# Splitting the first group's triangular inverse between VectorE and TensorE

## The chip, the cores and the metric

The kernel runs on one core of one Trainium2 chip. A core has five engines that each take their own queue of instructions: TensorE (PE, matrix products; PEld is its loading of weights), VectorE (DVE), ScalarE (ACT), GpSimd (POOL) and SyncE (SP, here only the issuing of transfers). The metric is the device time of one execution in microseconds (us). Line numbers such as L507 are those of the kernel before; the changed kernel has its own, some 40 to 60 higher from the place of the first edit on.

## What is computed

The reference is a linear attention with a delta rule, followed by a mixture of experts over slots. Only the first half is touched by the change.

```python
for t in range(S):                       # S = 768 tokens, B = 4, H = 8, D = 48
    kt, vt, bt = (k_n[:, :, t], v[:, :, t], beta[:, :, t, None])     # k_n: normed keys
    y[:, :, t] = np.einsum('bhd,bhde->bhe', q[:, :, t], state)
    v_old = np.einsum('bhde,bhd->bhe', state, kt)
    state = state + bt[:, :, :, None] * np.einsum('bhd,bhe->bhde', kt, vt - v_old)
...
logits = x @ phi                         # x: y as (3072, 384); 32 slots
d = softmax over tokens;  slot_input = d.T @ x;  relu(slot_input @ w1) @ w2 per expert
c = softmax over slots;   out = c @ slot_out
```

The 768 steps are worked in chunks of 32 tokens. Within a chunk the steps depend on each other through a lower triangular 32x32 system for each of the 32 pairs of batch and head. With its inverse T in hand, a chunk is a handful of matrix products: R = v minus keys times state, U = T R, state plus keys times U, and outputs from the state and from U.

## The kernel before, in words

**Chunks, slots and groups.** There are NCH = 24 chunks. The loop `for x in range(NCH)` treats one chunk in each turn, called a slot. Four chunks make a group (GC = 4, NG = 6), and one inverse covers a whole group: the 128 partitions hold 4 heads x 32 rows, and VectorE inverts for all of them at once. `U` = 8 pairs of batch and head-half lie in the free dimension of each chunk.

**The inverse, `invert(n)`.** `unit` and `clear` zero two scratch tiles on GpSimd (`tt`, and `nm` inside `prs`). `spread` (L325) transposes the products of keys with keys, `GQ`, in blocks of 32, `root` has ScalarE take the norms, and `norms` scales the system. `steps` is a list of small VectorE operations. The triangle is cut into halves of HC = 16: `ea`/`es` (an outer product at L368 and its subtraction at L373) solve both diagonal halves together; `ma`/`ms` and `la`/`ls` build the block that couples them, in `nm` and `T21`, and `join` (L410) copies it into `tt`. `back(half)` (L433) transposes half of the columns into `TT[n]`, as the solves want it. Before the first slot the steps of group 0 run in one go; those of later groups are dealt out over the four slots before they are needed, by `plan(n)` and the table `share`, in three places of each slot. A first argument of `put` weighs each step by its size.

**A chunk's slot.** In the order in which each engine's queue receives it: `rest` (state times keys into `psR`, and R, by VectorE or, where `turned_sign` holds, by a TensorE product with `minus`, L494, and a ScalarE copy, L498), `read` (state times queries, L481), `solve` (L507, with the matrices `Tb` that `solvers` has ScalarE make from `TT`, L458; ScalarE copies U, L510), then preparation of later chunks by `later(x, place)`, then `update` (L520, with the state's copy at L527) and `outputs` (L537, copied at L540). `Prep` turns keys and queries on TensorE (L261) into `KQ` (ScalarE copies at L270 and L277) and multiplies them (`products`, L290, copies at L294). Until slot 3 the table `ahead` names what is prepared where: q2 is query 2's turn, p2 its products, t8 and u8 the two halves of chunk 8's turns. All of these products share two PSUM buffers, the tag `pt`. `weights` masks the query products on GpSimd (L450), and `scale_v` scales the values there (L442).

**What sets the order.** The region is under a manual schedule: each engine runs its instructions in the order in which the code issues them, and waits by semaphores for its operands and for buffers. Transfers of keys, queries and values are issued by SyncE, four for each load (L93), in order too; a load into a buffer in use holds up those behind it.

**Routing.** `route(n, ...)` returns what a finished group contributes to the experts' slots, as lists by slot and place (`hook`). `shares` is four small VectorE operations (L638 to L641), `collect` adds up the slots' inputs. The weights of the experts are loaded during the later slots into what comes free; their products run after the last slot.

Of the kernel before, what the change touches and what calls it, by code (L numbers as in the profile page):

```python
# [9 lines left out]
F32 = mybir.dt.float32  # L10
AX = mybir.AxisListType
ALU = mybir.AluOpType
# [5 lines left out]
def kernel(  # L18
# [26 lines left out]
    nc = tc.nc  # L45
# [58 lines left out]
    def load_q(cc, eng=nc.sync):  # L104
        load(q, q_of(cc), cc, eng)
# [196 lines left out]
    def invert(n):  # L302
# [72 lines left out]
        def steps():  # L375

            pr, out = {}, []

            def put(size, f):
                out.append((60 + size, f))  # L380

            def ea(j):
                lb, tt, m, w = part(st["lb"]), part(st["tt"]), j + 1, HC - 1 - j
                pr["e", j] = outer("prE", [2, w, m], tt[:, :, j, 0:m].unsqueeze(2),
                                   lb[:, :, j, j + 1:HC].unsqueeze(3))

            def es(j):
                add(part(st["tt"])[:, :, j + 1:HC, 0:j + 1], pr["e", j], ALU.subtract)

            def ma(j):  # L390
                lb, tt, m = full(st["lb"]), full(st["tt"]), j + 1
                pr["m", j] = outer("prM", [HC, m], tt[:, j, 0:m].unsqueeze(1),
                                   lb[:, j, HC:C].unsqueeze(2))

            def ms(j):
                add(nm[:, :, 0:j + 1], pr["m", j], ALU.subtract)

            def la(j):
                a, b = full(st["tt"])[:, HC + j:C, HC + j].unsqueeze(2), nm[:, j, :].unsqueeze(1)
                if j == 0:  # L400
                    nc.vector.tensor_tensor(T21, a.broadcast_to([P, HC, HC]),
                                            b.broadcast_to([P, HC, HC]), op=ALU.mult)
                else:
                    pr["l", j] = outer(("prE", "prM")[j % 2], [HC - j, HC], a, b)

            def ls(j):
                add(T21[:, j:HC, :], pr["l", j], ALU.add)

            def join():
                nc.vector.tensor_copy(full(st["tt"])[:, HC:C, 0:HC], T21)  # L410

            for j in range(HC):
                last = j == HC - 1
                if not last:
                    put(2 * (j + 1) * (HC - 1 - j), lambda j=j: ea(j))
                put(HC * (j + 1), lambda j=j: ma(j))
                if not last:
                    put(2 * (j + 1) * (HC - 1 - j), lambda j=j: es(j))
                put(HC * (j + 1), lambda j=j: ms(j))
            for j in range(HC + 1):  # L420
                if j < HC:
                    put(HC * (HC - j), lambda j=j: la(j))
                if j > 1:
                    put(HC * (HC + 1 - j), lambda j=j - 1: ls(j))
            put(HC * HC, join)
            return out

        def back(half):

            if n not in TT:  # L430
                TT[n] = lp.tile([P, C, C], F32, name="TT", tag="TT", bufs=2)
            r = slice(half * HC, (half + 1) * HC)
            nc.vector.transpose(TT[n][:, :, r].rearrange("p c i -> p i c"), full(st["tt"])[:, r])  # L433

        return dict(unit=unit, clear=clear, spread=spread, root=root, norms=norms, back=back,
                    steps=steps())
# [128 lines left out]
    def route(n, Yn, yT, cs=range(GC), turn=None, behind=False):  # L565
# [160 lines left out]
    def drain(ls):  # L726
        for f in ls:
            f()
# [11 lines left out]
    PLACES = 3  # L740
    share = [(0.0, 0.05, 0.11), (0.0, 0.14, 0.15), (0.13, 0.10, 0.10), (0.12, 0.10, 0.0)]

    def plan(n):

        f = invert(n)
        at = [[[] for _ in range(PLACES)] for _ in range(GC)]
        todo, done, total = f["steps"], 0.0, 0.0
        whole = sum(t[0] for t in todo)
        norms = f["norms"]
        i = 0  # L750
        for c in range(GC):
            for p in range(PLACES):
                total += share[c][p] * whole
# [10 lines left out]
    nc.vector.tensor_reduce(msk, msk4, axis=AX.X, op=ALU.add)  # L764
    order = tc.manual_schedule()
    order.__enter__()

# [15 lines left out]
    f0["norms"]()  # L783
    pre[0].alone(1, 0)
    load_q(7)
    f0["clear"]()
    drain([t[1] for t in f0["steps"]])
    for i in range(2):
        f0["back"](i)
    pre[0].products(1, 2)  # L790
    scale_v(0)
    for cc in range(4, 8):
        pre[cc] = Prep(cc)
        pre[cc].alone(0, 1)
        pre[cc].alone(1, 0)
        if cc > 4:
            pre[cc - 1].products()
    load_q(1)
    load_k(8)
    load_q(2)  # L800
    load_q(8)
    load_q(3)
# [12 lines left out]
    f["unit"]()  # L815
    f["clear"]()
    routing, yT, two = {}, {}, {}


    def step(cc, kind):  # L820
# [61 lines left out]
    for x in range(NCH):  # L882
        n, c = divmod(x, GC)
        if c == 0 and n:
            routing[n - 1] = route(n - 1, Ys[(n - 1) % 2], yT[n - 1])

        def hook(name):
            for m in sorted(routing):
                at = x - GC * (m + 1)
                if at < len(routing[m]):  # L890
                    drain(routing[m][at].get(name, []))
            if x >= NCH - 2:
                ends(x, name)


        if x + AHEAD < NCH:
            load_k(x + AHEAD)
        for i in queries.get(x, (x + AHEAD,)):
            if i < NCH:
                load_q(i)  # L900
        if 0 <= x + 4 < NCH:
            load_v(x + 4)
        if 8 <= x < 8 + NKT:
            if x == 8:
                w0 = wpool.tile([P, NKT * F], F32, name="w0", tag="w0", bufs=1)
# [31 lines left out]
        later(x, 1)  # L937
        hook("mid")
# [239 lines left out]
```

## Time and profile before

| what | value |
|---|---|
| time, median of 3 runs | 314.1 us (313.29 to 319.79) |
| span of the profiled execution | 310.8 us, mean TensorE clock 0.945 |
| busy: PE / DVE / ACT / POOL | 84% / 70% / 55% / 51% |
| chain that ended last: PE / DVE / ACT | 47% / 24% / 16% |
| first group's inverse on VectorE, L368 to L410 | 19.2 to 39.6 us |
| first solve of slots 0, 1, 2, 3, 4 (L507) | 42.8, 57.3, 66.3, 75.3, 84.8 us |

Busy shares are means over the whole span, and the stages differ. The chain of waits goes back from the last instruction through whatever released each step, so that it says for each stretch of time which engine set the pace. The rows by stage give the clock that was granted to TensorE, 1.00 being full speed. A matrix product of 32-bit numbers shows as two records in the profile, so a group of 32 products is listed as x64.

### The profile page before, as it was taken

Reading aid. Unit: us, or ns where it says so; the run is one execution under the profiler, and the core shown is the slowest. Engines: PE = TensorE matmul, PEld = TensorE weight load, DVE = VectorE, ACT = ScalarE, POOL = GpSimd, SP = SyncE. Lnnn points to the kernel's source line nnn. Section 1 sums busy time; section 2 is a strip of 40 time slices with the busy share of each in tenths; the row PEclk is TensorE's granted clock in tenths of the full one; section 3 lists DMA queues with packets and bytes.
Section 4 is the critical chain, followed back from the end, with each engine's and each line's share of the span. In section 5 each row is a group of like instructions: output and inputs, shape, how many; then the busy total and the mean of one; then the engine's idle time right before and its main releaser. Section 6 shows DMA issues by size and latency. Waiting matters only on the chain.

```text
span 310.8 us, 16635 instructions
## 1 busy us (share of the span) xinstructions
PE 261.1 (84%) x7081; PEld 209.0 (67%) x7081; DVE 216.3 (70%) x807; ACT 171.7 (55%) x386; POOL 159.2 (51%) x336
## 2 busy tenths in 40 slices
PE   3996848998898988999988999796998878999981
PEld 2764636787787777777877877675877666447750
DVE  7689957969489995999579996999832223124341
ACT  3355236476777668578685678556576642211231
POOL 8969094861749957873789509999420000000000
PEclk9999566999999999999999999999799998999985
DMA  7765555434545444665431365668786599591387
GB/s 142 147 112 89 90 96 98 75 60 82 88 72 85 80 79 67 138 135 129 77 83 31 89 165 188 182 183 246 239 263 206 166 344 345 180 308 57 119 262 232
DMA packets 96378, 45.28 MB, mean 146 GB/s; under 512 B 75440, under 2 KB 89808, under 8 KB 96304
## 3 DMA queue, kind: packets, MB, share of 16 engines
q1 hardware_dynamic: 94512, 42.98, 55.3%
q0 software_dynamic: 704, 1.03, 1.5%
q8 instruction: 56, 0.92, 1.2%
q10 hardware_dynamic: 1088, 0.20, 0.3%
q14 instruction: 18, 0.15, 0.2%
HBM read 39.47 MB, written 4.72 MB: 142 GB/s over the span
## 4 chain that ended last, share of the span: by engine, by line
PE 47%; DVE 24%; ACT 16%; issue 3%; DMA 3%; SPq 2%; POOL 2%; DVEq 0%; POOLq 0%; ACTq 0%
DVE prs L368 9%; PE psR L507 6%; DVE prs L373 5%; PE psS L520 5%; PE pt L290 5%; ACT S L527 4%; PE pso L1061 3%; PE ph L1038 3%; PE pt L558 3%; PE pt L261 3%; DVE tt L373 3%; PE psY L537 2%; ACT dr L678 2%; PE psR L481 2%; PE po L1119 2%
## 5 line engine op out<-in xcount | busy, mean ns | idle before, releaser
L442 POOL TENSOR_SCALAR Vs<-Vs,nT 128x48 f32<-128x48 f32 x192 | 89.7, 491 | 22.9 <-DMA Vs<-in_v_dram 6.9
L373 DVE TENSOR_TENSOR prs<-prs 128x16 f32<-128x16 f32 (+15 forms) x186 | 55.8, 300 | 0.4
L450 POOL TENSOR_SCALAR_AFFINE_SELECT Abs<-GQ 32x256 f32<-32x256 f32 x96 | 48.5, 505 | 14.0 <-PE psY L537 9.2
L368 DVE TENSOR_TENSOR prs<-tt,lb 128x96 f32<-128x96 f32 (+21 forms) x186 | 47.8, 295 | 0.1
L527 ACT ACTIVATE S<-psS 48x768 f32<-48x768 f32 x46 | 36.9, 802 | 5.5 <-PE psS L520 5.0
L507 PE MATMUL psR<-R,Tbs 64*64 64x48 f32 x768 | 28.6, 226 | 11.8 <-ACT R L498 8.3
L507 PEld LDWEIGHTS psR<-R,Tbs 64*64 64x64 f32 x768 | 25.7, 140 | 15.6 <-ACT R L498 10.0
L290 PE MATMUL pt<-KQ 48*32 48x64 f32 (+1 forms) x1792 | 26.0, 234 | 5.4 <-ACT KQ L277 3.2
L510 ACT ACTIVATE U<-psR 128x384 f32<-128x384 f32 x24 | 11.8, 490 | 32.4 <-PE psR L507 27.2
L290 PEld LDWEIGHTS pt<-KQ 48*32 48x32 f32 x1792 | 21.0, 117 | 10.4 <-ACT KQ L277 5.0
L537 PE MATMUL psY<-U,Abs 64*64 64x48 f32 x768 | 27.4, 220 | 0.2 <-issue 0.2
L368 DVE TENSOR_TENSOR prs<-tt,prs 128x240 f32<-128x240 f32 (+14 forms) x90 | 27.0, 306 | 0.0
L537 PEld LDWEIGHTS psY<-U,Abs 64*64 64x64 f32 x768 | 24.3, 134 | 2.8 <-issue 0.7
L373 DVE TENSOR_TENSOR tt<-tt,prs 128x30 f32<-128x30 f32 (+7 forms) x90 | 26.0, 288 | 0.0
L458 ACT ACTIVATE Tbs<-TT,own 128x256 f32<-128x256 f32 x48 | 21.6, 501 | 5.9 <-DVE TT L433 5.9
L294 ACT ACTIVATE GQ<-pt 128x256 f32<-128x256 f32 (+1 forms) x56 | 16.9, 351 | 12.8 <-PE pt L290 12.5
L481 PEld LDWEIGHTS psR<-S,KQ 128*32 128x32 f32 x768 | 16.4, 112 | 8.8 <-ACT S L527 4.6
L481 PE MATMUL psY<-S,KQ 128*32 128x96 f32 x768 | 21.5, 246 | 1.0 <-issue 0.8
L481 PE MATMUL psR<-S,KQ 128*32 128x96 f32 x768 | 21.2, 253 | 1.0 <-ACT S L527 0.8
L558 PE MATMUL pt<-ident,Y 128*96 128x128 f32 x96 | 16.4, 294 | 6.4 <-ACT GQ L294 5.7
L500 DVE TENSOR_TENSOR R<-Vs,psR 128x384 f32<-128x384 f32 x14 | 7.7, 553 | 18.7 <-PE psR L481 7.1
L320 POOL MEMSET prs<- 128x256 f32 x6 | 1.9, 315 | 34.8 <-DVE prs L368 34.8
(230 smaller groups left out, 598.9 us busy)
## 6 DMA issues: line engine op xcount, KB each, us to landing
Q<-in_q_dram SPq DMA_DIRECT2D x96, 48.0 KB, 2.6
wKQ<-in_moe_w_dram SPq DMA_DIRECT2D x16, 256.0 KB, 3.9
Vs<-in_v_dram SPq DMA_DIRECT2D x80, 48.0 KB, 2.4
wGQ<-in_moe_w_dram SPq DMA_DIRECT2D x12, 256.0 KB, 4.8
Ka<-in_k_dram SPq DMA_DIRECT2D x40, 48.0 KB, 2.5
w<-in_moe_w_dram SPq DMA_DIRECT2D x6, 256.0 KB, 3.9
Ka<-in_moe_w_dram SPq DMA_DIRECT2D x8, 192.0 KB, 3.8
S<-in_moe_w_dram SPq DMA_DIRECT2D x8, 192.0 KB, 5.2
```

The lines of the kernel that those rows point to most:

```text
L290: nc.tensor.matmul(pg[g][rh, b], lhsT=kq[r, b, 0, rh], rhs=kq[r, b, a0:a1, rh], start=True, stop=True, skip_group_check=True)
L294: nc.scalar.activation(GQ[n][:, c, :, g, a0:a1], pg[g], ACT.Copy)
L368: nc.vector.tensor_tensor(pr, a.broadcast_to([P] + shape), b.broadcast_to([P] + shape), op=ALU.mult)
L373: nc.vector.tensor_tensor(dst, dst, pr, op=op)
L442: nc.gpsimd.tensor_scalar(Vt[cc][:, u], Vt[cc][:, u], nT[n][:, c * U + u:c * U + u + 1], None, op0=ALU.mult)
L450: nc.gpsimd.affine_select(out=Ab[cc % NT][r, :, h % 2, :].rearrange("p (b g) t -> p b g t", g=G), in_=GQ[n][r, c, :, :, 1, :], compare_op= ...
L458: nc.scalar.activation(Tb[cc % 2][:, :, x, :], TT[n][:, c * U:(c + 1) * U, :], ACT.Identity, scale=own[:, x:x + 1])
L481: nc.tensor.matmul(dst[hs[h], b].rearrange("p g d -> p (g d)"), lhsT=kq[:, b, a, hs[h]], rhs=old[:, h, b, :], start=((a == 1 or not turned ...
L507: nc.tensor.matmul(pw[half[y], u], lhsT=T[y][:, u], rhs=st["R"][half[y], u], start=(u == 0), stop=True, skip_group_check=True)
L527: nc.scalar.activation(new[r, :, :, g * D:(g + 1) * D], psS[r, :, 0:B * GD].rearrange("p h (b g e) -> p h b g e", b=B, g=G)[:, :, :, g], A ...
L537: nc.tensor.matmul(qs[half[y], b, g], lhsT=at[y][:, u], rhs=st["U"][half[y], u], start=False, stop=True, skip_group_check=True)
L558: nc.tensor.transpose(py[:, b, :], Yn[:, c, i + b, 0:GD], ident)
```

## The change

For group 0 alone, VectorE now solves only the two diagonal halves. The coupling block of each chunk is made by TensorE: `inner` multiplies the key products by the second half of the inverse, ScalarE copies the result with its sign turned, `outer` multiplies the first half's rows into it, and VectorE adds the result to `TT[0]`. For this the first half is also needed untransposed by columns: `rows` makes it in a scratch, `w0`, that the experts' weights use later. Chunk 0 is coupled ahead of slot 0, the other three in the slots before they are needed. The aim is a shorter stretch in which VectorE alone is at work ahead of slot 0.

Along with it, `spread` and `root` of group 1 move ahead of slot 0 and its steps get a table of their own, `first`; query 1's preparation moves into slot 0, and those of queries 2 and 3 later by a place or a slot; query loads are issued at other points; and `shares` of a group's routing moves from behind `collect(True)` to an earlier place of the same slot.

```diff
@@ steps()
+            if n == 0:
+                for j in range(HC - 1):
+                    put(2 * (j + 1) * (HC - 1 - j), lambda j=j: ea(j))
+                    put(2 * (j + 1) * (HC - 1 - j), lambda j=j: es(j))
+                return out
...
+        def rows(dst):
+            nc.vector.transpose(dst[:, :, 0:HC].rearrange("p c k -> p k c"),
+                                full(st["tt"])[:, :, 0:HC].rearrange("p i k -> p k i"))
...
+    class Coupling:
+        def each(self, lhsT, rhs):
+            p = pt([P, U, HC])
+            for u in range(U):
+                for h in range(4):
+                    r = slice(C * h, C * h + C)
+                    nc.tensor.matmul(p[r, u], lhsT=lhsT(r, u), rhs=rhs(r, u), start=True,
+                                     stop=True, skip_group_check=True)
+            return p
+        def inner(self):
+            p = self.each(lambda r, u: GQ[0][r, self.c, u // G, u % G, 0, :],
+                          lambda r, u: TT[0][r, self.c * U + u, HC:C])
+            nc.scalar.activation(self.sums[:, self.us], p, ACT.Copy, scale=-1.0)
+        def outer(self):
+            self.p = self.each(lambda r, u: self.rows[r, self.c * U + u],
+                               lambda r, u: self.sums[r, self.c * U + u])
+        def add(self):
+            o = TT[0][:, self.us, HC:C]
+            nc.vector.tensor_tensor(o, o, self.p, op=ALU.add)
@@ route()
-                    dict(sums=[lambda: slots((0, 1))], vec=[lambda: collect(True), shares]),
+                    dict(sums=[lambda: slots((0, 1))], act=[shares],
+                         vec=[lambda: collect(True)]),
@@ plan(), for n == 1
+    first = [(0.0, 0.10, 0.15), (0.0, 0.12, 0.13), (0.12, 0.10, 0.10), (0.10, 0.08, 0.0)]
@@ ahead of slot 0
+    w0 = wpool.tile([P, NKT * F], F32, name="w0", tag="w0", bufs=1)
...
+    nc.gpsimd.memset(w0[:, 0:C * C], 0.0)
...
-    f0["clear"]()
-    drain([t[1] for t in f0["steps"]])
-    for i in range(2):
-        f0["back"](i)
     pre[0].products(1, 2)
     scale_v(0)
+    load_k(8)
+    drain([t[1] for t in f0["steps"]])
+    f0["back"](1)
+    f0["rows"](rows11)
+    f0["back"](0)
+    couple = [Coupling(c, rows11, sums21) for c in range(GC)]
     for cc in range(4, 8):
         pre[cc] = Prep(cc)
         pre[cc].alone(0, 1)
+        if cc == 7:
+            couple[0].inner()
         pre[cc].alone(1, 0)
...
-    pre[7].products()
-    pre[1].alone(1, 0)
-    pre[1].products(1, 2)
+    couple[0].outer()
+    couple[0].add()
     weights(0)
     solvers(0)
+    pre[7].products()
+    couple[1].inner()
     scale_v(1)
...
     f["clear"]()
+    f["spread"]()
+    f["root"]()
...
-    ahead = {0: ("q2 p2", "t8 u8", "q3 p3"), 1: ("p8", "t9 u9", "p9"),
+    ahead = {0: ("q1 p1", "t8 u8", "q2 p2"), 1: ("p8", "q3 p3 t9 u9", "p9"),
@@ in slot x
         later(x, 0)
-        if x == 0:
-            f["spread"]()
-            f["root"]()
+        if x < GC - 1:
+            couple[x + 1].outer()
+            couple[x + 1].add()
...
         later(x, 1)
+        if x < 2:
+            load_queries()
+            couple[x + 2].inner()
```

More of the change, by code (lines that the diff above doesn't have):

```diff
@@ L433, in back, with __init__ @@
             nc.vector.transpose(TT[n][:, :, r].rearrange("p c i -> p i c"), full(st["tt"])[:, r])
+        def rows(dst):
+            nc.vector.transpose(dst[:, :, 0:HC].rearrange("p c k -> p k c"),
+                                full(st["tt"])[:, :, 0:HC].rearrange("p i k -> p k i"))
         return dict(unit=unit, clear=clear, spread=spread, root=root, norms=norms, back=back,
-                    steps=steps())
+                    steps=steps(), rows=rows)
+    class Coupling:
+        def __init__(self, c, rows, sums):
+            self.c, self.rows, self.sums = c, rows, sums
+            self.us = slice(c * U, (c + 1) * U)
+        def each(self, lhsT, rhs):
[16 more added lines that the diff above has]
+            nc.vector.tensor_tensor(o, o, self.p, op=ALU.add)
     def scale_v(cc):
@@ L752, in plan @@
             for p in range(PLACES):
-                total += share[c][p] * whole
+                total += (first if n == 1 else share)[c][p] * whole
                 while i < len(todo) and done + todo[i][0] / 2 < total:
@@ L764 @@
     nc.vector.tensor_reduce(msk, msk4, axis=AX.X, op=ALU.add)
+    w0 = wpool.tile([P, NKT * F], F32, name="w0", tag="w0", bufs=1)
+    rows11 = w0[:, 0:C * C].rearrange("p (c k) -> p c k", k=C)
+    sums21 = w0[:, C * C:C * C + C * HC].rearrange("p (c i) -> p c i", i=HC)
+    nc.gpsimd.memset(w0[:, 0:C * C], 0.0)
     order = tc.manual_schedule()
@@ L794 @@
         pre[cc].alone(0, 1)
+        if cc == 7:
+            couple[0].inner()
         pre[cc].alone(1, 0)
+        if cc < 7:
+            load_q(cc - 3)
         if cc > 4:
             pre[cc - 1].products()
-    load_q(1)
-    load_k(8)
-    load_q(2)
     load_q(8)
-    load_q(3)
     load_k(9)
@@ L897, with load_queries @@
             load_k(x + AHEAD)
-        for i in queries.get(x, (x + AHEAD,)):
-            if i < NCH:
-                load_q(i)
+        def load_queries():
+            for i in queries.get(x, (x + AHEAD,)):
+                if i < NCH:
+                    load_q(i)
+        if x > 1:
+            load_queries()
         if 0 <= x + 4 < NCH:
@@ L903 @@
         if 8 <= x < 8 + NKT:
-            if x == 8:
-                w0 = wpool.tile([P, NKT * F], F32, name="w0", tag="w0", bufs=1)
             load_w1(0, [x - 8], w0[:, (x - 8) * F:(x - 7) * F])
@@ L937 @@
         later(x, 1)
+        if x < 2:
+            load_queries()
+            couple[x + 2].inner()
         hook("mid")
```

## The prediction

> **What bounds the kernel now.** I read the chain of waits first, in order of time. Columns are start and length in microseconds, engine, tile, line.
>
> ```profile
> 18.35 0.69 DVE lb L350
> 19.25 0.21 DVE prs L368 x2
> ...
> 39.31 0.29 DVE tt L410
> 39.60 1.83 DVE TT L433 x2
> 41.45 0.91 ACT Tbs L458 x2
> 42.36 0.39 ACT R L498
> 42.79 1.95 PE psR L507 x32
> ```
>
> From 18.35 to 41.43 us VectorE alone is the chain: group 0's inverse, 94 instructions at L368, L373, L401 and L410, then two transposes. Slot 0's first solve (L507) starts 0.45 us after ScalarE's R copy ends. By the same line of the chain and PE's timeline the solves of slots 1 to 4 start at 57.3, 66.3, 75.3 and 84.8.
>
> The second view is busy time by stage (length, PE, PEld, DVE, ACT, POOL, granted clock, DMA share, GB/s), cut where the clock changes:
>
> ```profile
> 27.40:31.00 3.60, 1.43 (x69) 1.13 (x69) 3.60 (x18) 1.59 (x4) 3.44 (x7) 0.98 0.47 77
> 31.00:34.50 3.50, 2.81 (x101) 2.15 (x102) 3.43 (x13) 1.47 (x4) 0.00 (x0) 0.50 0.63 105
> 34.50:37.70 3.20, 3.20 (x86) 2.06 (x70) 3.20 (x16) 0.45 (x2) 0.00 (x0) 0.50 0.53 89
> 37.70:41.50 3.80, 0.90 (x44) 0.68 (x36) 3.73 (x16) 0.05 (x1) 2.52 (x7) 0.95 0.48 82
> 41.50:45.00 3.50, 2.21 (x34) 2.12 (x35) 1.82 (x2) 1.45 (x4) 3.22 (x9) 0.50 0.55 97
> 45.00:48.00 3.00, 1.96 (x70) 1.43 (x69) 0.00 (x0) 1.46 (x6) 2.54 (x8) 0.50 0.56 95
> 48.00:50.70 2.70, 2.70 (x32) 2.37 (x35) 2.17 (x7) 2.17 (x5) 1.70 (x4) 0.50 0.48 86
> 50.70:54.00 3.30, 2.38 (x52) 1.92 (x48) 3.30 (x24) 2.39 (x4) 0.48 (x1) 0.91 0.61 95
> ```
>
> Twice, after a stretch in which TensorE had little to do, its clock halves: about 31 to 38 and 41.5 to 50.7 us. So slot 0 runs at half rate for most of its length, and takes 14.5 us where slots 1 and 2 take 9.0.
>
> The third is PE's timeline, for what already lies under the inverse and for prices:
>
> ```profile
> 29.12 0.63 PE L261 MATMUL psR<-ident,Q 128*128 128x128 f32 x4 [1.80 <-DMA Q<-in_q_dram]
> ...
> 34.99 1.65 PE L494 MATMUL psR<-Vs,minus 128*128 128x384 f32 x2
> 36.56 1.38 PE L481 MATMUL psR<-S,KQ 128*32 128x96 f32 x32
> ...
> 46.47 0.89 PE L290 MATMUL pt<-KQ 48*32 48x32 f32 x64 [0.69 <-ACT KQ L277]
> ...
> 54.25 0.76 PE L290 MATMUL pt<-KQ 48*32 48x32 f32 x64 [1.17 <-ACT KQ L277]
> ```
>
> Slot 0's state products (L494, L481) and query 1's preparation are finished by 38.6, hidden below VectorE. 64 records of 32 columns cost 0.76 us at full clock and 0.89 at half; the same 64 records with 64 columns cost 0.86 at full. That price hardly follows the columns.
>
> **What the Trainium skill says.** "TensorE: Matmul & The Clock Gate", Part 1: half rate is what TensorE falls to after an idle window of about 3.4 us and leaves after a busy one. The table agrees (0.50 and about 1.00, nothing between but at the changes). The same page, Architectural detail: ScalarE and VectorE take their queues strictly in order; the trace shows no instruction overtaking. "VectorE: DVE Perf Modes", The TRN2 errata: each instruction pays a fixed latency, whatever its size. The trace agrees: 0.17 us for 16 elements, 0.42 for 256, so about 0.15 plus 1.04 ns an element. That page's The DRAIN you can't avoid says a semaphore between two VectorE operations costs nothing extra; here the dependent 128x32 operations of L347 and L348 last 0.19 and start 0.23 apart in group 1, so I add 0.035 each.
>
> **The change, part by part.**
>
> *Group 0 on VectorE.* 64 of 94 instructions go (the coupling and its join); 30 stay, each waiting for the one before. Their sizes sum to 2 x 1360 elements: 30 x 0.15 + 2720 x 1.04 ns = 7.3 us, plus 30 x 0.035 = 1.05. Before, independent neighbours overlapped; that is lost. GpSimd's weights(0) lies at 23.1 to 25.6 in both kernels; there single operations grow from 0.28 to 0.52 and the stage loses about 0.9. From 19.2 the chain ends at 28.5. Lower bound without the last two terms 26.5; upper bound 30. Then three transposes at about 1.0 (L433's median 1.045): back(1) to 29.5, rows to 30.5, back(0) to 31.5.
>
> *Coupling products, new.* Four inner and four outer, each 32 matmuls (64 records) of 16 columns. No row shows it. Half of the 0.89 row gives 0.43 as a floor, 0.9 is the ceiling; because 32 and 64 columns cost nearly the same I take 0.76 at full and 0.9 at half clock. The ScalarE copy of 128x128 is about 0.27 (L294), the add on VectorE about 0.3.
>
> *Up to the first solve.* inner(0) 29.5 to 30.25, before query 7's turn, whose data lands at 29.1 anyway; turn to 30.9; chunk 6's products to 32.1; ScalarE frees the first PSUM buffer at 32.5 (only two, "pt"); outer(0) to 33.4, add to 33.7, Tbs to 34.6. So the solver matrix comes 7 us before the 42.36 of now. But TensorE is not ready: chunk 7's products need the buffer that the add frees, 33.75 to 35.2 at half clock (1.44); inner(1) to 36.5; L494 to 38.15 (1.65); L481 to 39.2 as the clock returns; R to 39.7; solve at 39.9. ScalarE's root for group 1, now queued ahead of R, needs GQ7 (35.9), a 1.95 transpose and ssq, so ends at 38.65: just hidden. At full clock throughout the solve comes at 38.2, with the root last. I take 38.9, a gain of 3.9 against 42.8, because the clock should return on the way.
>
> *Slot 0.* Solve 1.1; query 1 and its products, formerly hidden, to 3.1; outer(1) waits for a GQ copy, to 4.15; add to 4.5; Tbs to 5.4; ScalarE's two KQ copies behind it to 6.5, which inner(2) needs the first of, 6.0 to 6.75; update to 7.75; ScalarE's S, Y and query 2's copy to 10.4; products to 11.2; L494, L481 and R 2.0: next solve at 13.3, against 14.5 at half clock.
>
> *Slot 1.* Chunk 8's products to 1.95, outer(2) to 3.15, Y's turn to 3.8; query 3 has moved here, and its copy waits behind yTs and Tbs to 5.8, so TensorE stands 1.3 us; its products to 6.55; chunk 9's turns to 7.8; inner(3) to 8.7; update 9.7; ScalarE's S until 11.35; state products; solve at 12.9 against 9.0.
>
> *Slot 2.* outer(3) sits ahead of the turns: 9.0 + 0.75 = 9.7. Slot 3 is as before.
>
> The sum from first to fourth solve is 35.9 against 32.5 (75.3 - 42.8), so 3.4 of the 3.9 is paid back, and 0.5 us remains at slot 3, give or take the 0.9 of the two ends.
>
> *Adds in VectorE's queue.* add(2) stands behind group 1's norms (2.7) and eight double steps (about 6), started at 4.5 in slot 0: done at 13.2, before slot 1 asks at 3.2. Hidden. Should they run late, the add holds Tbs, one PSUM buffer and query 3's turn.
>
> *Group 1 earlier, new shares.* Its transpose fell at 41.28; now 36. Not on the path: the inverse ended at 78.4, and slot 4's Tbs waited for ScalarE until 83.83. Moving query loads: SyncE's queue issues four in 1.93 us and is busy to 47 either way; chunk 8's data lands near 39, before slot 0 asks for it at about 43. The scratch memset (about 1 us) lies in GpSimd's early idle time. All three count nothing.
>
> *Shares of the routing.* Four VectorE operations (163.33 to 164.39, 1.06 us) move from behind the first collect to where VectorE waits for the root:
>
> ```profile
> 157.49 0.35 DVE L343 RECIPROCAL rn<-nrm 128x32 f32<-128x32 f32 x1 [1.57 <-ACT nrm L336]
> ...
> 163.33 0.28 DVE L638 TENSOR_REDUCE sm<-el 128x4 f32<-128x128 f32 x1
> ...
> 164.09 0.37 DVE L641 TENSOR_TENSOR Call<-el,sm 128x128 f32<-128x128 f32 x1
> ...
> 193.13 0.35 DVE L343 RECIPROCAL rn<-nrm 128x32 f32<-128x32 f32 x1 [1.37 <-ACT nrm L336]
> ```
>
> The idle 1.57 and 1.37 hold them, and the chain is VectorE's from 157.5 to 181.3 and 193.1 to 216. Two groups make at most 2.1, with slots 8 to 11 (PE's chain) perhaps 2.6; if TensorE is next, 0.8. I take 2.2.
>
> Together 0.5 + 2.2 = 2.7: 314.1 - 2.7 = 311.4, told as 311.
>
> **Rivals.** *The start is kept whole.* The new matmuls cost their floor, saving about 0.33 for each of the five in the slots (1.7) and for the products beside them as much; the clock stays full, first solve at 37.5. Then slots of 12.0, 12.1 and 9.4 put the fourth solve at 71: 4.3 plus 2.6 of shares makes 307, or 305 if query 3's stall vanishes. For: TensorE stands idle for some 8 us in 26 to 42.8 now (busy time in stretches of 2 us), so room exists. Against: two PSUM buffers and the 0.76 row. *Half clock again in slot 0.* If waits on buffers keep TensorE from a busy window until about 46, slot 0 loses some 3 us: fourth solve at 77.5, total 315. For: from 41.5 to 48 it stayed low at 64% busy (2.21 + 1.96 of 6.5). Against: there is no 4 us hole any more. *Slower than before.* The adds fall behind the inverse on VectorE; with 3 us lost in each of slots 0 to 2 beyond the sum above, 311 + 9 = 320 to 322. For: VectorE is 91% busy in 25 to 45. Against: 64 instructions less.
>
> **How the numbers follow.** 311: 0.47. Kept whole, about 306: 0.33. Half clock, 315: 0.11. Slower, 321: 0.09. The two percent bounds are 307.8 and 320.4, so faster 0.33, same 0.58, slower 0.09. Low 304.5 takes in the second case with its floor, high 316 the third; what lies beyond is the slower case and a tail of the second.
>
> **What would show it.** VectorE's group 0 between 26.5 and 30 us; first solve between 38 and 40; slot 1 near 13 us with a TensorE wait on ScalarE's KQ ahead of query 3's products; fourth solve at 74 to 76; L679 to L682 ahead of the norms, and the reciprocal not later. A fourth solve below 72 or slots of 10 would make me wrong on the fast side; adds waiting on VectorE, or a clock of 0.5 past 42, on the slow one.

## The result, and the profile after

The changed kernel takes 323.7 us (median of 4 runs, 321.46 to 325.49) against 314.1 us for the kernel before on the same chip. The ratio is 1.029 with a 95% interval of 1.021 to 1.038: slower. The forecast was 311; nearest to what happened is the rival that was given 0.09, 320 to 322, though not for the reason it named. The executions of one kernel scatter by some 3%, so a ratio here and below compares the undisturbed ones on the same chip and needn't be the quotient of two medians, while the slot times of a kernel are read from one execution, which in the experiments a_fill_hole, coupling_only, coupling_fill and b_fill_shares was one of its slower ones (327.4, 327.8, 324.4 and 311.8 us).

The page of the changed kernel, busy time by engine and the chain of waits by engine:

```profile
PE 274.6 (85%) x7593; PEld 220.9 (68%) x7593; DVE 205.0 (63%) x748; ACT 173.8 (54%) x390; POOL 162.0 (50%) x336
...
PE 44%; DVE 24%; ACT 16%; issue 5%; POOL 5%; DMA 2%; SPq 1%; DVEq 0%; POOLq 0%; ACTq 0%
```

VectorE did lose work (216.3 us before, 205.0 now), and TensorE is busy for longer, 274.6 us against 261.1. No engine's share tells why the end moved by 12.9 us in the profiled pair (span 323.7 against 310.8; the medians are 9.6 apart). The starts of the first solves do. Each column after the first is the time from one solve to the next:

| kernel | first solve (slot 0) | slot 0 | slot 1 | slot 2 | fourth solve |
|---|---|---|---|---|---|
| before | 42.8 | 14.5 | 9.0 | 9.0 | 75.3 |
| predicted | 38.9 | 13.3 | 12.9 | 9.7 | 74.8 |
| changed | 43.0 | 18.3 | 18.0 | 9.65 | 88.95 |

At the fourth solve 13.7 us are lost; the later slots carry that along within 2 us. The first solve didn't come earlier, and slots 0 and 1 took 10.1 us more than predicted.

The chain of waits of the changed kernel up to the first solve (start, length, engine, tile, line; a group of 32 products may show fewer than 64 records here, and pieces under 0.05 us are left out):

```profile
18.85 0.69 DVE lb L350
...
29.64 1.06 DVE TT L439
30.70 0.14 issue
30.84 1.05 PE pt L461 x51
31.89 1.05 PE psR L261 x4
32.94 1.11 PE pt L290 x62
34.05 0.50 issue
34.55 1.08 PE pt L461 x64
35.66 0.30 DVE TT L477
36.00 1.31 PE pt L290 x61
37.31 0.37 ACT GQ L294
37.73 1.05 PE pt L461 x64
38.78 1.58 PE psR L535 x2
40.35 1.44 PE psR L522 x32
41.79 1.28 PE psY L522 x32
43.07 1.55 PE psR L548 x32
```

VectorE hands over at 30.7 instead of 41.4. From there the chain is TensorE's: everything it used to do under the inverse (chunk 7's products, L535, L522) is still in front of it, now behind the coupling, and each piece at half speed. The stages, cut as before:

```profile
27.40:31.00 3.60, 0.16 (x13) 0.19 (x17) 3.29 (x11) 0.00 (x0) 3.60 (x10) 0.92 0.46 72
31.00:34.50 3.50, 3.05 (x132) 2.44 (x127) 1.45 (x2) 1.30 (x4) 1.50 (x5) 0.50 0.61 102
34.50:37.70 3.20, 2.67 (x128) 2.18 (x128) 0.29 (x1) 1.54 (x5) 0.00 (x0) 0.50 0.49 80
...
50.70:54.00 3.30, 3.30 (x71) 3.09 (x65) 3.30 (x24) 1.47 (x3) 2.31 (x6) 0.50 0.42 60
```

In the first row TensorE's busy time (the second number) is 0.16 of 3.60 us: the hole that lay at 38 to 42 us before now lies at 27 to 31. The clock, third number from the end, is 0.50 straight after it. It returns at about 44, and falls again from 47.5 to 61 and from 68 to 78.

TensorE's timeline in slot 1 of the changed kernel (start, length, line, tiles, then the idle time before it and what ended that):

```profile
63.68 0.68 PE L461 MATMUL pt<-w 32*32 32x16 f32 x59 [0.46 <-ACT GQ L294]
65.41 0.24 PE L461 MATMUL pt<-w 32*32 32x16 f32 x5 [1.05 <-issue]
...
68.18 0.89 PE L290 MATMUL pt<-KQ 48*32 48x32 f32 x64 [1.48 <-ACT KQ L277]
...
71.33 1.05 PE L461 MATMUL pt<-TT,GQ 32*32 32x16 f32 x64
72.31 1.82 PE L561 MATMUL psS<-U,Ka 32*112 32x96 f32 x32
74.06 1.94 PE L578 MATMUL psY<-U,Abs 64*64 64x48 f32 x32
```

Query 3's products wait 1.48 us for ScalarE's copy, and a coupling group is cut in two by 1.05 us in which TensorE waited for nothing that the profile shows. From 68 us on the clock is low again: L561 and L578 take 1.82 and 1.94 us here, where 1.04 and 1.14 are their prices at full clock in slot 1 of the kernel before.

### The profile page after: what moved, and what is told of

Read it like the earlier page. It is cut to its first block, busy times and chain, and to the rows that moved or that the text cites. A ratio compares the mean times of both kernels' runs of the same rounds, so it can differ in the third digit from the quotient of the medians.

```text
span 323.7 us, 17606 instructions
## 1 busy us (share of the span) xinstructions
PE 274.6 (85%) x7593; PEld 220.9 (68%) x7593; DVE 205.0 (63%) x748; ACT 173.8 (54%) x390; POOL 162.0 (50%) x336
## 4 chain that ended last, share of the span: by engine, by line
PE 44%; DVE 24%; ACT 16%; issue 5%; POOL 5%; DMA 2%; SPq 1%; DVEq 0%; POOLq 0%; ACTq 0%
DVE prs L368 8%; PE psR L548 5%; PE pt L290 5%; DVE prs L373 5%; ACT S L568 4%; DVE tt L373 4%; PE pso L1120 3%; PE ph L1097 3%; PE psS L561 3%; PE pt L599 3%; PE pt L261 2%; POOL Abs L491 2%; PE pt L461 2%; PE psR L522 2%; PE psY L578 2%
## 5 line engine op out<-in xcount | busy, mean ns | idle before, releaser
L483 POOL TENSOR_SCALAR Vs<-Vs,nT 128x48 f32<-128x48 f32 x192 | 94.2, 514 | 19.4 <-DMA Vs<-in_v_dram 10.7
L491 POOL TENSOR_SCALAR_AFFINE_SELECT Abs<-GQ 32x256 f32<-32x256 f32 x96 | 46.3, 483 | 35.8 <-ACT GQ L294 26.2
L373 DVE TENSOR_TENSOR prs<-prs 128x16 f32<-128x16 f32 (+15 forms) x155 | 46.5, 300 | 0.3
L368 DVE TENSOR_TENSOR prs<-tt,lb 128x96 f32<-128x96 f32 (+21 forms) x170 | 42.4, 284 | 0.5
L290 PE MATMUL pt<-KQ 48*32 48x64 f32 (+1 forms) x1792 | 27.6, 238 | 6.3 <-ACT KQ L277 3.5
L290 PEld LDWEIGHTS pt<-KQ 48*32 48x32 f32 x1792 | 21.7, 119 | 11.5 <-ACT KQ L277 5.2
L578 PE MATMUL psY<-U,Abs 64*64 64x48 f32 x768 | 29.1, 227 | 0.3 <-issue 0.3
L578 PEld LDWEIGHTS psY<-U,Abs 64*64 64x64 f32 x768 | 25.9, 142 | 2.8 <-issue 0.9
L522 PE MATMUL psY<-S,KQ 128*32 128x96 f32 x768 | 22.8, 256 | 4.6 <-issue 3.8
L373 DVE TENSOR_TENSOR tt<-tt,prs 128x30 f32<-128x30 f32 (+7 forms) x90 | 24.2, 269 | 0.5
L522 PEld LDWEIGHTS psR<-S,KQ 128*32 128x32 f32 x768 | 17.5, 117 | 9.2 <-ACT S L568 4.6
L522 PE MATMUL psR<-S,KQ 128*32 128x96 f32 x768 | 22.5, 263 | 1.0 <-ACT S L568 0.8
L522 PEld LDWEIGHTS psY<-S,KQ 128*32 128x32 f32 x768 | 18.7, 116 | 5.6 <-issue 4.6
L368 DVE TENSOR_TENSOR prs<-tt,prs 128x240 f32<-128x240 f32 (+14 forms) x75 | 21.8, 297 | 0.0
```

Source lines behind the costliest of these rows:

```text
L290: nc.tensor.matmul(pg[g][rh, b], lhsT=kq[r, b, 0, rh], rhs=kq[r, b, a0:a1, rh], start=True, stop=True, skip_group_check=True)
L368: nc.vector.tensor_tensor(pr, a.broadcast_to([P] + shape), b.broadcast_to([P] + shape), op=ALU.mult)
L373: nc.vector.tensor_tensor(dst, dst, pr, op=op)
L491: nc.gpsimd.affine_select(out=Ab[cc % NT][r, :, h % 2, :].rearrange("p (b g) t -> p b g t", g=G), in_=GQ[n][r, c, :, :, 1, :], compare_op= ...
L522: nc.tensor.matmul(dst[hs[h], b].rearrange("p g d -> p (g d)"), lhsT=kq[:, b, a, hs[h]], rhs=old[:, h, b, :], start=((a == 1 or not turned ...
L578: nc.tensor.matmul(qs[half[y], b, g], lhsT=at[y][:, u], rhs=st["U"][half[y], u], start=False, stop=True, skip_group_check=True)
```

## The experiments

Two theories were on the table. *Clock*: the change itself is priced about right, and the loss is TensorE's clock, halved by the hole that moved and by thin stretches in the slots. *Work in the queues*: the coupling and the moved queries cost what they cost in slots where TensorE is next in line, at any clock. The idle products used below multiply the identity by itself into a part of a PSUM tile that nothing reads; they add no result.

### Keep the clock up, in either kernel

`a_fill_hole`, the changed kernel:

```diff
         if cc == 7:
+            fill(24)          # 24 products ident x ident
             couple[0].inner()
```

> The changed kernel with 24 idle 128x128 products on TensorE (into unused PSUM columns) ahead of inner(0), where it stood idle from 26.7 to 30.8 us. Clock theory: the loss comes from TensorE's half rate, which that hole sets off; then the clock stays near 1.0 to about 40 us, the first solve comes at 38 to 40 instead of 43.0, and the time falls by 3 to 8 us to 316 to 321. Work theory: the added coupling products and the query turns moved into slots 0 and 1 make them long whatever the clock; then the fourth solve stays near 88 us and the time at 322 to 325.

`a_fill_slots` also fills where the slots wait for ScalarE: 4 products behind query 1's turn, 8 behind query 3's, and 4 ahead of `couple[2].inner()`.

> As the run before, and 4, 4 and 8 such products also in slots 0 and 1, ahead of the waits for query 1's copy, for inner(2) and for query 3's copy. Clock theory: slots 0 and 1 run at full clock and take 13 to 14 us each instead of 18.3 and 18.0, the fourth solve comes near 76 and the time near 311 to 314. Work theory: still 17 us or more per slot, and the fillers only add to it: 323 or more.

`b_fill_holes`, the kernel before:

```diff
         if cc == 7:
+            fill(10)          # ahead of query 7's turn
...
         read()
+        if x == 0:
+            fill(24)          # ahead of the first solve
```

> The kernel before with idle products in its own two holes: 10 ahead of query 7's turn, 24 between slot 0's query product and its solve. Clock theory: slot 0, at half clock from 41.5 to 50.7, shortens from 14.5 to 10.5 or 11.5, and the time falls from 314 to about 310. If TensorE's clock is not what makes slot 0 long, no change: 313 to 315.

| kernel | first solve | slot 0 | slot 1 | slot 2 | fourth solve | time, ratio to before |
|---|---|---|---|---|---|---|
| a_fill_hole | 45.6 | 18.1 | 17.1 | 9.65 | 90.5 | 323.3, 1.026 (1.016 to 1.037) |
| a_fill_slots | 44.5 | 14.8 | 15.0 | 10.9 | 85.2 | 318.1, 1.018 (1.010 to 1.027) |
| b_fill_holes | 43.9 | 11.5 | 9.0 | 9.15 | 73.5 | 309.3, 0.990 (0.980 to 1.000) |

Filling the hole alone gave nothing. TensorE ran at full clock through the filler, and lost it 4 to 6 us behind it in the stretch of coupling and prep; by stage, a_fill_slots, which has the same filler:

```profile
34.72:38.14 3.42, 2.26 (x162) 1.81 (x165) 0.37 (x2) 1.66 (x5) 0.00 (x0) 0.99 0.45 77
38.14:41.55 3.41, 2.08 (x48) 1.12 (x37) 2.02 (x2) 0.72 (x3) 0.00 (x0) 0.50 0.45 79
...
44.96:48.38 3.42, 3.06 (x110) 2.78 (x108) 0.00 (x0) 1.46 (x4) 0.00 (x0) 1.00 0.50 89
```

In the first row TensorE idles for 1.16 us: 0.46 us until ScalarE's copy has emptied a PSUM buffer, 0.17 until VectorE's add, and 0.54 in a pause that ends on nothing the profile records. In a_fill_hole the stretch before the fall was busy for 1.97 of 3.41 us. So the hole isn't the only cause of the low clock; the short waits and pauses among the coupling products are a second. The filler is also longer than the hole: VectorE's first transpose ends at 30.6 us in both kernels, and `inner(0)` starts at 32.05 and 32.48, against 30.84 in the changed kernel. The two runs therefore don't show what a filler of the right length would do ahead of slot 0; coupling_fill, below, has one (`inner(0)` at 30.85).

With the slots filled too (a_fill_slots) the clock is 1.00 from 45 us on, and slots 0 and 1 fall from 36.3 to 29.8 us, though TensorE has 16 products more to do; slot 2 is 1.2 us longer, with 1.1 us of pauses in it. So the half clock is worth about 6.5 us in slots 0 and 1. But the kernel before gains from a full clock as well: its slot 0 shrinks from 14.5 to 11.5 us. By stage, b_fill_holes:

```profile
44.55:47.96 3.41, 2.37 (x90) 1.93 (x87) 0.00 (x0) 1.90 (x7) 3.34 (x9) 1.00 0.40 71
47.96:51.38 3.42, 3.27 (x74) 2.71 (x72) 3.11 (x14) 3.38 (x8) 1.47 (x4) 1.00 0.51 85
```

With the clock held in the slots of both, the changed kernel's fourth solve is still 11.6 us behind (85.2 against 73.5), where it was 13.7 without the fillers. Its slots 0 to 2 take 40.6 us against 29.6. Of these 11 us some 1.4 are the fillers' own, by an estimate from the waits that they stand in: 0.13 and 0.24 us more than the waits for query 1's and query 3's copies in the changed kernel, and 0.99 ahead of `couple[2].inner()`, where TensorE didn't wait.

Neither forecast for a_fill_slots came true as it stood, and both theories hold a part: the clock explains much of why the numbers of the prediction were missed, and the work in the queues is why the change loses even where the clock is equal. In the total times the second is clear, since the intervals of a_fill_slots and b_fill_holes lie apart; what the fillers gain in either kernel alone is not clear of the noise.

### The change in halves

`moves_only` is the changed kernel without the coupling; group 0 is solved whole on VectorE, with `spread` and `root`, the queries and the shares at their new places. Group 0's `clear`, which the changed kernel doesn't need, comes back behind `scale_v(0)`:

```diff
-            if n == 0:
-                for j in range(HC - 1):
-                    ...
-                return out
...
     scale_v(0)
     load_k(8)
+    f0["clear"]()
...
-            couple[0].inner()
...
-    couple[0].outer()
-    couple[0].add()
...
-    couple[1].inner()
```

> The changed kernel with all its moves (query 1 to 3's preparation, group 1's spread and root ahead of slot 0, its own shares, the routing's shares), but group 0's inverse wholly on VectorE again and no coupling products. If the moves make slots 0 and 1 long: first solve near 45 (R waits behind the root), those slots 15 to 18 and 11 to 13 us, time 318 to 323. If the coupling products on TensorE are the cost: slots 14 and 10 to 11, time 314 to 317.

`coupling_only` is the kernel before with the coupling and nothing else: query 1 prepared ahead of slot 0, queries 2 and 3 in slot 0, group 1's `spread` and `root` in slot 0, the shares behind the collect.

```diff
-    ahead = {0: ("q1 p1", "t8 u8", "q2 p2"), 1: ("p8", "q3 p3 t9 u9", "p9"),
+    ahead = {0: ("q2 p2", "t8 u8", "q3 p3"), 1: ("p8", "t9 u9", "p9"),
```

> The kernel before with group 0's coupling on TensorE, chunk by chunk as in the change, and none of the moves (query 1 stays ahead of slot 0, query 3 in slot 0, spread and root in slot 0, shares as before). If the coupling products are the cost: first solve 43 to 45, slots 0 to 2 some 16, 14 and 10 us, time 319 to 324. If the moves are: slot 1 back to about 10.5, time 313 to 317.

`coupling_fill` is the same with 16, 2, 3 and 2 idle products at four places ahead of slot 0.

> As coupling_only, with 16, 2, 3 and 2 idle 128x128 products in TensorE's waits ahead of slot 0, so that its clock stays up. Clock theory: first solve 39 to 41, below the 43.9 of the kernel before with fillers, and slot 0 at 13 us; time 309 to 313. Work theory: the slots stay long by the five coupling products and their waits, the fourth solve comes at 76 or later, behind the 73.5 of the kernel before with fillers, and the time is above 311.

| kernel | first solve | slot 0 | slot 1 | slot 2 | fourth solve | time, ratio to before |
|---|---|---|---|---|---|---|
| moves_only | 49.7 | 14.5 | 11.9 | 9.0 | 85.1 | 325.0, 1.032 (1.015 to 1.048) |
| coupling_only | 45.25 | 18.3 | 12.9 | 9.6 | 86.0 | 324.6, 1.026 (1.009 to 1.042) |
| coupling_fill | 44.15 | 17.4 | 12.8 | 12.2 | 86.55 | 319.9, 1.006 (1.001 to 1.011) |

The time of moves_only says little on the moves: in this mixture the `clear` of group 0 stood behind GpSimd's scaling of chunk 0, for which VectorE waited 3.07 us, and R stood behind group 1's root; TensorE waited 12.90 us for R and started slot 0 at 49.7. That is an artefact of the experiment. Its slots can be read all the same. Slot 1 ran at full clock and took 11.9 us against 9.0, with query 3's wait in it, 1.52 us for ScalarE's copy: the moves cost 2.9 us there. Slot 1 of coupling_only, at full clock but for its first quarter of a microsecond, took 12.9: the coupling costs 3.9. (Slot 1 of hole_work, below, which also has the coupling and not query 3, took 12.4 at full clock.) The two together on 9.0 make 15.8, and a_fill_slots, which has both, shows 15.0. Slot 1 of the changed kernel is thus about 9.0 of old work, 6 us of new, and 3 us of half clock.

The slots of coupling_fill, with half clock in parts of slots 0 and 2, are those of an execution of 324.4 us among 314.8 to 326.1, and don't go with its ratio. The ratio says that the coupling with fillers is still no faster than the kernel before without any, which is what the work theory expected of it (above 311 us).

The coupling also leaves its mark on VectorE, which takes its queue strictly in order, as the Trainium skill says for it ("TensorE: Matmul & The Clock Gate", Architectural detail). VectorE's timeline, the two longest waits among the four adds of coupling_only:

```profile
50.18 0.29 DVE L477 TENSOR_TENSOR TT<-TT,pt 128x128 f32<-128x128 f32 x1 [10.31 <-PE pt L461]
...
66.76 0.29 DVE L477 TENSOR_TENSOR TT<-TT,pt 128x128 f32<-128x128 f32 x1 [10.22 <-PE pt L461]
```

At its four adds VectorE waits for 25.6 us in all, with group 1's inverse behind them in its queue. The steps that it missed come later, and with them R of slot 2: TensorE waits 1.63 us there for it, in the timeline of coupling_only:

```profile
76.38 1.14 PE L548 MATMUL psR<-R,Tbs 64*64 64x48 f32 x32 [1.63 <-DVE R L541]
```

In the changed kernel, where group 1's transpose and root come ahead of slot 0, the same wait is 0.18 us. That fits group 1's earlier start, which wasn't tried alone; VectorE's own wait stays (9.85 us at the third add).

### The shares alone

```diff
-                    dict(sums=[lambda: slots((0, 1))], vec=[lambda: collect(True), shares]),
+                    dict(sums=[lambda: slots((0, 1))], act=[shares],
+                         vec=[lambda: collect(True)]),
```

> The kernel before with the shares of the routing moved to the earlier place, and nothing else. My prediction's step: 0.8 to 2.6 us less, 312. If VectorE's wait for the root isn't long enough, or TensorE is the bound in slots 8 to 19, nothing: 314.

Measured: 313.3 us, ratio 0.993 (0.989 to 0.997), about 2.1 us. VectorE's timeline of b_shares:

```profile
156.46 0.28 DVE L638 TENSOR_REDUCE sm<-el 128x4 f32<-128x128 f32 x1
...
158.12 0.35 DVE L343 RECIPROCAL rn<-nrm 128x32 f32<-128x32 f32 x1 [0.57 <-ACT nrm L336]
```

The four operations fit into the wait, which shrinks by 1.00 us from the 1.57 of before, and the reciprocal starts 0.63 us later than there, by as much as this execution's first solve was already late. But this first group gains almost nothing: from its solve to the next it is 9.58 us against 9.75, as TensorE had waited only 0.43 us for R there. Nearly the whole gain lies in slot 16, which takes 7.89 us instead of 9.86. Slot 17's solve waits 0.77 us for VectorE's R instead of 2.33; TensorE's timelines, before and b_shares:

```profile
202.54 1.13 PE L507 MATMUL psR<-R,Tbs 64*64 64x48 f32 x32 [2.33 <-DVE R L500]
201.02 1.14 PE L507 MATMUL psR<-R,Tbs 64*64 64x48 f32 x32 [0.77 <-DVE R L500]
```

This part of the change is a gain, by the mechanism that was argued, in one of the two places that it was expected in.

### Another order ahead of slot 0

If TensorE's hole is the trouble, the work that the change left behind the coupling can go into it. `hole_work` puts slot 0's state products and R and query 1's preparation ahead of `couple[0].inner()`, `couple[1].inner()` and group 1's root behind the first solve, and query 3's turn back into slot 0:

```diff
         if cc == 7:
+            slot0 = chunk(0, Ys[0])
+            slot0[0]()
+            slot0[2]()
+            pre[1].alone(1, 0)
+            pre[1].products(1, 2)
             couple[0].inner()
```

> The changed kernel with its TensorE queue reordered: slot 0's state products, R's copy and query 1's preparation go into the hole ahead of inner(0), where TensorE waited for VectorE from 26.7 to 30.8; inner(1) and the root come after slot 0's solve; query 3 goes back to slot 0. The coupling products stay. Order theory: what was lost ahead of slot 0 is that work hidden below the inverse was queued behind it; then the first solve comes at 35 to 38 instead of 43.0, the fourth at 70 to 74 if the clock holds, the time at 308 to 313. If the coupling products themselves are too dear: the first solve comes early too, but slots 0 to 2 sum to 38 or more and the time is 314 or more.

`hole_work_fill` has 2, 2, 3, 4 and 3 idle products more, at five places in and behind the hole.

> As hole_work, with 2, 2, 3, 4 and 3 idle 128x128 products in TensorE's remaining waits up to slot 0. If the clock is what is left: full clock to the fourth solve, slots 0 to 2 sum to 33 to 36, the fourth solve before 72, time 307 to 311. If not: within 1 percent of hole_work.

`hole_state` leaves query 1's preparation where it was, behind chunk 7's products:

> The changed kernel with slot 0's two state products and R made ahead of the coupling products, in the idle time under VectorE's inverse, and query 1's preparation behind chunk 7's products (so TensorE's queue meets no late load there); chunk 1's first coupling product and group 1's root stand behind slot 0's solve, query 3's turn is back in slot 0. Theory (the first solve is lost to TensorE's order: the state products, the first product of chunk 1's coupling and the root stand ahead of it): TensorE's idle stretch ahead of the first coupling product shrinks from 4.1 to about 1.5 us, the clock is near full up to the first solve, which starts at 36 to 38 us instead of 43.0. Rival (the clock falls anyway, since what is queued there is too thin): the clock is 0.50 from about 34 on and the first solve comes at 39 to 41. On the slots: if the half clock was all that the slots lost, the fourth solve comes 36 us after the first at full clock, at 72 to 74, total 309 to 312; if the coupling itself makes slots 0 and 1 long in the in-order queues, the fourth solve comes 40 us or more after the first, at 77 or later, total 313 to 318.

| kernel | first solve | slot 0 | slot 1 | slot 2 | fourth solve | time, ratio to before |
|---|---|---|---|---|---|---|
| hole_work | 44.3 | 18.7 | 12.4 | 10.3 | 85.8 | 323.7, 1.015 (1.007 to 1.022) |
| hole_work_fill | 46.8 | 19.4 | 12.0 | 10.6 | 88.9 | 324.2, 1.032 (1.026 to 1.038) |
| hole_state | 40.1 | 20.6 | 12.35 | 10.3 | 83.4 | 322.4, 1.023 (1.015 to 1.032) |

hole_work's ratio stands for about 319 us of the kernel before, whose 21 executions on that chip took 311 to 322; set against the five shortest (311 to 315) it would be about 1.035. No order comes near what its theory asked for (307 to 313 us). hole_work opened a new hole in place of the old one. TensorE's timeline:

```profile
33.54 1.09 PE L261 MATMUL psR<-ident,Q 128*128 128x128 f32 x4 [4.22 <-DMA Q<-in_q_dram]
```

Query 1's load stands in SyncE's queue behind those of keys, is issued from 29.9 us on, and TensorE, in order, waits 4.22 us for it. hole_work_fill has the same wait, and its fillers couldn't bridge it. hole_state avoids it:

```profile
28.54 0.84 PE L522 MATMUL psY<-S,KQ 128*32 128x96 f32 x32
31.24 0.72 PE L461 MATMUL pt<-TT,GQ 32*32 32x16 f32 x64 [1.86 <-DVE TT L439]
...
33.87 0.33 PE L461 MATMUL pt<-w 32*32 32x16 f32 x17 [0.46 <-ACT GQ L294]
35.18 0.83 PE L461 MATMUL pt<-w 32*32 32x16 f32 x47 [0.98 <-issue]
```

The hole is 1.86 us, the state products are out of the way, and the first solve starts at 40.1, 2.9 us sooner than in the changed kernel and 2.7 sooner than before. That is less than the theory asked for (36 to 38): the clock falls at 34.95, after a stretch busy for 2.16 of 3.41 us, and stays at 0.50 until 62. That is what the rival expected. And it is of no use. Slot 0 takes 20.6 us; the fourth solve is 43.2 us behind the first, and the total isn't told apart from that of the changed kernel. Here an earlier first solve didn't shorten the slots behind it.

### What beats both

The fillers of b_fill_holes and the moved shares together, without the coupling: `b_fill_shares`, and the same kernel again with more executions, `b_fill_shares_5`.

> The kernel before with the idle products in its two holes and the routing's shares moved: both gains add up if they lie in different stages: 309.3 less about 2, so 307 to 308, two percent below the kernel before. If not: 309 to 310.

> The kernel before with 10 idle 128x128 products ahead of query 7's turn and 24 between slot 0's read and its solve, and the shares of the routing moved as in the change; the same kernel as b_fill_shares, in more rounds, for an interval. Theory (the clock and the shares are separate gains of about 1 percent and 0.7 percent): ratio to the kernel before 0.975 to 0.988, fourth solve near 73.2. Rival (the fillers only shift the low clock elsewhere): ratio 0.99 to 1.00.

The first gave 311.65 us (median of 4) against 316.5 for the kernel before, with no interval, and a fourth solve at 73.2. The second gave 309.8 us, ratio 0.980 (0.973 to 0.987), the lowest ratio of the study. Its interval lies below that of b_shares (0.989 to 0.997, on another chip), so the fillers have a part in it, and its mean clock was 0.955 to 0.971 in six executions, against 0.899 to 0.937 in the eleven of the kernel before on that chip. In its profiled execution the clock fell nevertheless from 45 to 59 us, slot 0 took 15.7 and the fourth solve came at 77.4; so the fillers don't guarantee the full clock in that stage, and how much of the 2% is theirs in each execution is not shown.

## Why the prediction was wrong, step by step

- **Group 0 on VectorE** was right within its bounds. Predicted 19.2 to 28.5, with an end between 26.5 and 30; measured 19.7 to 29.6, of which 0.5 is a later start.
- **Price of the coupling products** was right at full clock: 0.76 taken, 0.79 and 0.73 measured (the changed kernel's groups at 47.01 and 80.37 us), and low at half clock: 0.9 taken, 1.05 measured.
- **Up to the first solve** failed: 43.0 for 38.9. Of these 4.1 us, 1.3 are there when `inner(0)` starts, at 30.84 for 29.5, since VectorE began and ended later. Some 2.5 are the clock: `inner(0)` and query 7's turn, priced at full clock with 0.75 and 0.65, took 1.05 each; L535 and the two groups of L522 ran at half clock to the end and took 4.2 us for 3.4; and the walk's own 39.9 had been cut to 38.9 with the words "because the clock should return on the way". The clock was 0.50 from 30.4 to 44, and "a clock of 0.5 past 42" was among the signs that the prediction gave for being wrong. The prediction took its walk from 29.5 on and didn't ask what TensorE would do from 26.7 to 30.8. It did nothing, since the first coupling product was next in its queue and all else stood behind it. The half-clock rival was dismissed with "there is no 4 us hole any more"; the hole was 4.10 us long, just elsewhere. Nor does it take such a hole: in the prediction's own table the fall at 31.0 follows a stretch that was busy for 1.43 of 3.60 us, and that the table agreed with an idle window was read wrongly.
- **Slots 0 and 1** failed in the same way, and worse: 13.3 and 12.9 were worked out at full clock and measured 18.3 and 18.0 at mostly half. With the clock held, slot 0 is 14.8 and slot 1 15.0, with 8 idle products in each, so the full-clock sums were low by at most 1.5 and 2.1 us. A part of that is the pauses named "issue" inside groups of small products, 0.44 us in slot 0 and 0.83 in slot 1 of a_fill_slots, which no step of the sum had. So the step that failed is the clock: the sum put half clock at nothing behind the first solve, and it cost 3.5 and 3.0 us of the 5.0 and 5.1 that these slots were longer than predicted.
- **The comparison itself** was unfair: the changed kernel's slots at full clock were set against the old ones at half. The kernel before at full clock has 11.5, 9.0 and 9.15 us, and against these even the predicted 13.3, 12.9 and 9.7 lose 6.3 us. The prediction credited the change with a clock that the change doesn't give. This is the step to learn from, since the row of before that shows slot 0 at 0.50 was on its own page.
- **Adds in VectorE's queue**: right for TensorE. VectorE was ready for add(2) at 55.85, 12.8 us into slot 0 (13.2 predicted), well ahead of TensorE. What it missed is the wait the other way: VectorE stood 9.85 us at that add with group 1's steps behind it. Here that cost 0.18; in coupling_only 1.63.
- **Query 3's wait**: 1.3 predicted, 1.48 measured. **Slot 2**: 9.7 and 9.65. **Slot 3 as before**: 9.5 in both. **Group 1 earlier**: no cost seen. **Shares**: 2.2 predicted within 0.8 to 2.6; 2.1 measured alone. That the sum fits is partly luck: two groups were to give about 1.06 each, and in the traces one gives 2.0 and the other 0.2.
- **The sum**: the predicted fourth solve was 74.8, the measured one 88.95. Of the 14.1 us between, 4.1 are the first solve and 10.1 slots 0 and 1 (5.0 and 5.1). Holding the clock in the slots gives 6.5 of the 10.1 back.

The "slower" rival came nearest in size, by adding 3 us in each of three slots, but gave the adds as the reason. The half-clock rival had the mechanism, with its "waits on buffers keep TensorE from a busy window", and charged it to slot 0 alone.

What stays open is what makes the pauses of 0.4 to 1.3 us at the coupling products. They end on nothing that the profile records; shorter ones (0.2 to 0.5 us) lie inside other groups of small products too. From 26 to 90 us all such idle time sums to 1.6 us in the changed kernel and to 4.7 in a_fill_slots, where the same products run at full clock, to 0.8 and 0.2 in b_fill_shares and b_fill_shares_5, and there is none in the kernel before, in b_fill_holes and in moves_only. So most of it comes with the coupling, whatever makes it. The DMA records of the changed kernel show no packet at all in the one of slot 1 (64.3 to 65.5 us), so no recorded transfer explains it. A coupling in fewer, larger products wasn't tried.

## What to carry to other kernels

When work leaves the engine that sets the pace, ask at once what the next engine does meanwhile: here a hole of 4.1 us on TensorE was followed by 13.7 us at half clock, and all the work in that stretch was paid at half speed. Price the kernel before and the kernel after at the same clock, and count a clock that comes back as a gain of its own that could be had without the change. And a block that is divided into small products with a copy and an add between them costs its waits in every in-order queue it passes: here two groups of 0.73 us made a slot of 9.0 us into one of 12.9.

## What the runs showed of the hardware

The Trainium skill has TensorE's clock fall "after ≥1 idle window (~3.4µs)" ("TensorE: Matmul & The Clock Gate", Part 1). The time scale agrees: all changes of clock in these traces lie on a grid of 3.41 us. But the window needn't be idle. Cut along that grid, the changed kernel's stages are:

```profile
27.01:30.42 3.41, 0.00 (x0) 0.00 (x0) 3.07 (x11) 0.36 (x1) 3.41 (x9) 1.00 0.45 74
30.42:33.83 3.41, 2.99 (x132) 2.64 (x132) 2.03 (x3) 0.88 (x2) 2.08 (x6) 0.50 0.63 102
...
40.66:44.07 3.41, 3.41 (x83) 3.13 (x74) 0.00 (x0) 0.58 (x2) 0.00 (x0) 0.50 0.51 85
44.07:47.49 3.42, 2.38 (x143) 1.98 (x142) 0.00 (x0) 1.53 (x4) 0.30 (x1) 1.00 0.61 94
47.49:50.90 3.41, 3.41 (x105) 2.94 (x92) 2.86 (x10) 1.99 (x4) 3.13 (x7) 0.50 0.54 82
```

The first fall follows a stretch with no product at all, the second one that was busy for 2.38 of 3.42 us (70%). In 14 profiled executions, cut in this way between 18 and 88 us, each of the 23 falls follows a stretch that was 0 to 70% busy, and none follows a fuller one. The reverse doesn't hold: 13 stretches of 46 to 70% were not followed by a fall, so busy time as the profile counts it doesn't decide it alone. Three stretches that were 84 to 88% busy (30.42 to 40.66 here) also didn't bring the clock back; a full one did (40.66). Each of the 28 returns in these stretches follows a stretch that was 98 to 100% busy, though not every full one brings it back (47.49 here). For this kernel that means a slot whose waits add up to about a third of 3.4 us may be halved in speed, and that is how a change which adds waits of half a microsecond each can come to cost 3 us a slot.
